# A list scheduler for the feed-forward work of a fused attention, mixture and ELU kernel; PSUM banks that sum on between reads

## The chip, the core and the metric

The kernel runs on one core of one Trainium2 chip. The metric is device time in microseconds (us) of one execution. A core has five instruction queues that run side by side, each strictly in its written order: PE (matrix products), DVE and POOL (elementwise work), ACT (copies and activation functions, which also may issue DMAs) and SP, which here issues nearly all DMAs. A queue whose first instruction waits holds everything behind it.

## The reference, cut to what matters

```python
def _attn_ref(q, k, v):               # 2 x 8 heads, 1152 keys, 576 pooled queries, depth 64
    q_pool = q.reshape(B, H, S // 2, 2, D).mean(axis=3)
    attn = softmax(scale * q_pool @ k.T)
    return attn @ v                   # becomes x: 1152 tokens x 512
def _moe_ref(x, domain_probs, w1, w2):  # 4 experts, 512 -> 1024 -> 512
    p = domain_probs / (domain_probs.sum(-1, keepdims=True) + 1e-09)
    for e in range(E):
        out += p[:, e:e + 1] * (np.maximum(x @ w1[e], 0.0) @ w2[e])
def _moe2_ref(x, w_in, w_out):        # 512 -> 2048 -> 512, weights are 64-bit floats
    h = x @ w_in
    g = np.where(h > 0.0, h, np.exp(np.minimum(h, 0.0)) - 1.0)
    return g @ w_out
```

## The kernel before

**Stages.** Attention comes first and is not touched: its instructions stand on every engine in the same order in both kernels. Then come twelve groups of feed-forward work, each for 512 hidden columns: groups 0 to 7 are the four experts (two groups each, ReLU), groups 8 to 11 the ELU network. G1 = 8 is the first ELU group. The output of groups 0 to 7, summed in `acc`, is the input x of groups 8 to 11.

**The two products of a group.** The first one (512 to 512) is made by seven products of quarter matrices instead of eight, numbered 1 to 7, each for two halves s of its 576 tokens. TURNS is the order of the seven. Such a product (i, s) is 12 matmuls of 288 columns: two output halves, two contraction chunks, and three matmuls each, since every float32 operand is kept as a rounded high part and a low rest (h and l in the names), and high x high, low x high and high x low are summed. The hidden values are sums of the seven products: quarter 2 is p1+p2, 3 is p1+p6+p5+p3, 7 is p1+p6+p7+p5, 4 is p1+p6+p7-p4 (the numbers name the product that ends each). The second product (512 to 512) goes by six blocks (b, m), three token blocks b by two output halves m, each 24 matmuls of 384 columns. Both go through `product`, so all these matmuls bear one line, L877.

**What stands around the products.** `first` (L908 on) lets ACT copy p1 to `u0`; DVE adds the later products to `u0`, `u1`, `u2` (names u) and makes the hidden quarter in a tile `c`; ACT takes the ReLU of c as the high part `hh` (L890), DVE the low part `hl` (L891). Two PSUM buffers `ps1` serve all products, so a product can start only when the one two places before it has been read. For a block, DVE scales with the token's probability (`t`, L956) and POOL adds to `acc` (L957). Weights of the next group are split by ACT (L363, high) and POOL (L366, low; `sum` are the quarter sums).

**Narrowing.** The ELU weights come as 64-bit floats. `narrow(k)`, 32 steps in all, turns 512 columns into float32: one ACT instruction (L815), six DVE instructions (L816 to L832), one POOL sum (L835), a store to DRAM, and the load of the next 64-bit tile `d`, of which there is one. A step is written as one piece by `step`, so its six DVE instructions stand together, the first waiting for the load of `d`.

**Order.** Attention is ordered by a list scheduler (`order_of`). The feed-forward work is written by hand loops: product, its readers, and pieces of weight work from a list `pend`, two or one at a time. Narrowing steps stand after product 1 and after blocks with m = 0.

**The change of stage.** At g = G1 `split` and `combine_x` turn `acc` into the seven x operands, 1152 wide pieces (two chunks of 576 tokens) at a time, on ACT and DVE.

## Time and profile before

| what | value |
| --- | --- |
| median of 3 runs | 1065.26 us (1059.65 to 1066.82) |
| the profiled execution | 1059.69 us, span of its trace 1057.7 us |
| PE busy | 868.8 us (82%) |
| DVE busy | 644.8 us (61%) |
| POOL busy | 501.9 us (47%) |
| ACT busy | 403.2 us (38%) |
| mean granted clock of PE | 0.927 of full speed |

A trace shows when each instruction ran, what ended an engine's idle time (the releaser), and what clock PE was granted. Busy time of PE counts a matmul at a lower clock as longer, so a busy PE need not be a fast one. The rows below are copied from the views of this one execution; times in them count from its first instruction.

### The profile page before, as it was taken

What the parts mean: (1) busy time and instruction counts of PE and PEld (TensorE: products, weight loads), DVE (VectorE), ACT (ScalarE), POOL (GpSimd) and SP (SyncE); (2) the same over time, 40 slices, a digit from 0 to 9 for tenths busy, and PEclk for the clock granted to TensorE, in tenths of its full rate; (3) what the DMA queues carried; (4) which work ended last, traced back from release to release, by engine and by line L of the source; (5) the groups of instructions that cost most, each with busy time, mean ns of one, the idle gap of its engine ahead of it and who ended that gap; (6) DMA issues with size and microseconds to landing.
All of it is one profiled execution on the core that took longest, in us unless ns stands there. A gap on an engine that the chain in (4) does not pass through costs nothing.

```text
span 1057.7 us, 14469 instructions
## 1 busy us (share of the span) xinstructions
PE 868.8 (82%) x5470; PEld 791.1 (75%) x5470; DVE 644.8 (61%) x927; ACT 403.2 (38%) x816; POOL 501.9 (47%) x460
## 2 busy tenths in 40 slices
PE   8999999999596867958769598595865697988978
PEld 7777777776596867948669587595854597887978
DVE  8767786767555747567466574665756714436362
ACT  7777786775322213122121221212213344324140
POOL 4244333633325373563744637446375455536361
PEclk9999999999898998989979799897996699898989
DMA  7998787511412223222241222412221201102002
GB/s 240 190 177 182 191 177 178 103 45 46 161 48 76 92 89 117 61 60 90 72 140 47 73 81 65 157 36 84 82 59 41 79 1 40 41 1 80 1 1 90
DMA packets 48357, 95.02 MB, mean 90 GB/s; under 512 B 14368, under 2 KB 26144, under 8 KB 45344
## 3 DMA queue, kind: packets, MB, share of 16 engines
q1 hardware_dynamic: 48288, 94.11, 32.7%
q8 instruction: 43, 0.70, 0.3%
q14 instruction: 26, 0.21, 0.1%
HBM read 64.37 MB, written 10.84 MB: 71 GB/s over the span
## 4 chain that ended last, share of the span: by engine, by line
PE 44%; DVE 22%; DMA 10%; POOL 8%; issue 8%; ACT 7%; SPq 1%; DVEq 0%; ACTq 0%; POOLq 0%
PE p L877 26%; PE s L593 6%; PE t L655 5%; PE s L678 5%; DMA d<-in_va 4%; DMA d<-in_vb 3%; DVE c L366 3%; DVE nt L820 2%; DVE hl L891 2%; POOL sum L366 2%; DVE u L366 2%; DVE nt L823 2%; DMA acc<-xo 2%; POOL nt L835 2%; DVE e L902 2%
## 5 line engine op out<-in xcount | busy, mean ns | idle before, releaser
L877 PE MATMUL p<-hl,w2h 128*128 128x384 f32 x576 | 193.7, 336 | 4.7 <-POOL hl L906 4.7
L877 PE MATMUL p<-hh,w2h 128*128 128x384 f32 x576 | 194.1, 337 | 3.3 <-DVE t L956 3.1
L877 PE MATMUL p<-hh,w2l 128*128 128x384 f32 x576 | 193.1, 335 | 0.0
L877 PE MATMUL p<-XH,h 128*128 128x288 f32 x192 | 67.5, 352 | 90.4 <-DVE c L366 85.0
L957 POOL TENSOR_TENSOR acc<-acc,t 128x768 f32<-128x768 f32 x42 | 80.3, 1912 | 102.1 <-DVE t L956 102.1
L604 DVE TENSOR_REDUCE st<-s 128x1 f32<-128x512 f32 (+1 forms) x144 | 105.5, 751 | 18.6 <-PE s L593 15.2
L877 PEld LDWEIGHTS p<-XH,h 128*128 128x128 f32 x192 | 43.1, 225 | 96.3 <-DVE c L366 85.0
L593 PE MATMUL s<-K,Q 128*128 128x320 f32 (+1 forms) x480 | 110.1, 356 | 4.5 <-DVE xo L363 2.6
L877 PEld LDWEIGHTS p<-hl,w2h 128*128 128x128 f32 x576 | 108.7, 189 | 5.8 <-POOL hl L906 5.8
L877 PEld LDWEIGHTS p<-hh,w2h 128*128 128x128 f32 x576 | 108.6, 188 | 5.9 <-DVE t L956 5.3
L877 PEld LDWEIGHTS p<-hh,w2l 128*128 128x128 f32 x576 | 108.7, 189 | 0.0
L610 ACT ACTIVATE e<-s,st 128x512 f32<-128x512 f32 (+1 forms) x144 | 106.4, 747 | 5.6 <-DVE st L604 3.5
L363 ACT CAST h<-sum 128x512 fp32r<-128x512 f32 x48 | 29.7, 620 | 184.7 <-POOL sum L366 184.7
L366 POOL TENSOR_TENSOR l<-sum,h 128x512 fp32r<-128x512 f32 x48 | 62.9, 1311 | 75.2 <-ACT h L363 75.2
L877 PE MATMUL p<-K,h 128*128 128x288 f32 x384 | 81.8, 307 | 19.6 <-DVE u L366 8.1
L655 PE MATMUL t<-ident,e 128*128 128x128 f32 x648 | 94.1, 276 | 3.4 <-ACT e L610 2.5
L835 POOL TENSOR_TENSOR nt<-nt,ne 128x512 f32<-128x512 f32 x32 | 40.9, 1277 | 117.4 <-DVE ne L832 72.4
L655 PEld LDWEIGHTS t<-ident,e 128*128 128x128 f32 x648 | 75.4, 140 | 24.3 <-issue 7.4
L890 ACT ACTIVATE hh<-c 128x576 fp32r<-128x576 f32 x64 | 43.9, 685 | 128.1 <-DVE c L366 128.1
L891 DVE SCALAR_TENSOR_TENSOR hl<-c,hh 128x576 fp32r<-128x576 f32 x64 | 59.2, 925 | 53.6 <-ACT hh L890 53.6
L593 PEld LDWEIGHTS s<-K,Q 128*128 128x128 f32 x480 | 74.0, 190 | 11.3 <-DVE xo L363 3.0
L877 PEld LDWEIGHTS p<-K,h 128*128 128x128 f32 x384 | 64.5, 197 | 21.9 <-ACT u L923 8.3
(103 smaller groups left out, 1989.0 us busy)
## 6 DMA issues: line engine op xcount, KB each, us to landing
w<-in_wb SPq DMA_DIRECT2D x8, 1024.0 KB, 4.8
d<-in_va SPq DMA_DIRECT2D x16, 512.0 KB, 3.9
w<-nt SPq DMA_DIRECT2D x32, 256.0 KB, 2.6
d<-in_vb SPq DMA_DIRECT2D x16, 512.0 KB, 4.5
w<-w SPq DMA_DIRECT2D x8, 1024.0 KB, 4.9
Q<-q SPq DMA_DIRECT2D x28, 288.0 KB, 6.2
w<-in_wa SPq DMA_DIRECT2D x7, 1024.0 KB, 4.8
v<-in_v SPq DMA_DIRECT2D x16, 288.0 KB, 5.9
```

The costliest lines, as they stand in the source:

```text
L363: (nc.scalar.copy if e == "ACT" else engines[e].tensor_copy)(out, a)
L366: engines[e].tensor_tensor(out=out, in0=a, in1=b, op=op)
L593: nc.tensor.matmul(out=t[:, j], lhsT=q[:, o : o + P], rhs=ks[p % 2][:, y, c : c + PARTS[z][1]], start=k == x == 0, stop=2 * k + x == last,)
L604: nc.vector.tensor_reduce(out=nm[b, z], in_=s_t[b, z], axis=AX.XY, op=ALU.max, negate=True)
L610: nc.scalar.activation(et[b % NP][:, part(z)].rearrange("p (j k) -> p j k", j=PARTS[z][0]), s_t.pop((b, z)), AF.Exp, bias=nm.pop((b, z)), ...
L655: nc.tensor.transpose(t[:, c * P : c * P + P], et[b % NP][:, (3 * u + c) * P : (3 * u + c + 1) * P], ident)
L678: nc.tensor.matmul(out=tb[i, h][64 * z : 64 * z + 64, :HQ], lhsT=raws[i, "v"][:, c, :], rhs=pt[i % 2][:, c, half(z)], start=c == cs[0], st ...
L835: nc.gpsimd.tensor_tensor(out=t, in0=t, in1=e, op=ALU.add)
L877: nc.tensor.matmul(out=ps, lhsT=w[a][:, c, m * P : m * P + P], rhs=x[b][:, c], start=c == a + b == 0, stop=c == cs - 1 and a == 1,)
L890: nc.scalar.activation(oh, c, AF.Relu)
L891: nc.vector.scalar_tensor_tensor(out=ol, in0=c, scalar=0.0, in1=f(oh), op0=ALU.max, op1=ALU.subtract)
L957: nc.gpsimd.tensor_tensor(out=o, in0=o, in1=t, op=ALU.add)
```

## The change

The hand loops are replaced by a second list scheduler. `ffn_ops` writes every piece of feed-forward work as an operation: the engines it may run on with a duration in ns, what it needs, a due time taken from a plan of PE's products, and what buffer it takes or gives back. `ffn_order` then picks, again and again, the ready operation that can start first, by due time where several can, and the kernel is recorded in that order. Letters: F a product, P a block, u the copy of a partial sum, c a whole quarter, r and l its high and low part, t and a the scaling and the sum into acc, s h o the first weights (sum, high, low), C L the second weights, W Z D p loads, N a narrowing step's nine parts, H Y T the x operands, n e w x the ELU.

Four things change in the work itself. Product 6 sums on in the PSUM bank of product 1, then 7, then 4, and product 3 in that of 5; between them ACT copies the bank (u), so that PE must wait for that copy before it adds the next product. The eight additions that DVE made for each half of a group become three (c) and ACT makes three copies instead of one. Narrowing is issued in single instructions between others. The PSUM is four tiles of two banks that products and blocks share, with three tiles c and three tiles t. The x operands at the change of stage are made in halves of 576 elements, some on POOL. Weights and low parts of groups 8 to 11 may go to DVE instead of POOL, and the first load of second weights is issued by ACT. In groups 1 to 7 and 9 to 11 the order of products is 1, 2, 6, 7, 4, 5, 3.

```diff
--- before.py
+++ after.py
...
+FREE = dict(PE=0, DVE=13000, ACT=3000, POOL=6000, SP=15000)
+BUSY = dict(PE=0, DVE=75, ACT=85, POOL=30, SP=0)
+SEEN = dict(PE=200, DVE=40, ACT=40, POOL=40, SP=0)
+LATE_X = 15500
+PACE = 11600
+NARROW = [
+    dict(ACT=650), dict(DVE=830), dict(DVE=1200), dict(DVE=430), dict(DVE=690), dict(DVE=430),
+    dict(DVE=690), dict(POOL=1300), dict(SP=350),
+]
+HALF = {2: (0, 1), 3: (0, 0), 7: (1, 0), 4: (1, 1)}
...
+    for key in plan:
+        g = key[1]
+        if key[0] == "F":
+            i, s = key[2:]
+            need = [prev, ("o", g, i), ("Y", g, i, s)]
+            need += {6: [("u", g, 1, s)], 7: [("u", g, 6, s)], 4: [("u", g, 7, s)], 3: [("c", g, 7, s)]}.get(i, [])
+            last = {1: 4, 5: 3, 2: 2}.get(i)
+            op(key, dict(PE=1592), need, begin[key], takes=last and "ps")
+        else:
+            _, g, b, m, z = key
+            need = [prev] + [("L", g, c) for c in range(4)]
+            for j in range(384 * b // 288, (384 * b + 383) // 288 + 1):
+                need += [("l", g, q, j % 2) for q in HALF if HALF[q][1] == j // 2]
+            op(key, dict(PE=4162 if z == 2 else 2081), need, begin[key], takes="ps")
+        prev = key
...
+                if q in (2, 3, 7):
+                    need = {2: [src, ("u", g, 1, s)], 3: [src, ("u", g, 6, s)], 7: [("u", g, 7, s), ("F", g, 5, s)]}[q]
+                    hold = begin["F", g, 5, s] if q == 2 and turns[g][1] == 2 else nxt[3] if q == 7 else 1 << 40
+                    give = [] if q == 7 else [("ps", ("F", g, {2: 2, 3: 5}[q], s))]
+                    src = ("c", g, q, s)
+                    op(src, dict(DVE=755), need, min(due, hold - 800), takes="c" if q != 7 else None, gives=give)
+                    give = [("c", ("u", g, 7, s) if q == 7 else src)]
+                else:
+                    give = [("ps", ("F", g, 1, s))]
+                if g < G1:
+                    op(("r", g, q, s), dict(ACT=660), [src], due + 1000)
+                    op(("l", g, q, s), dict(DVE=755), [("r", g, q, s)], due + 1700, gives=give)
...
+    for k in range(8 * (NG - G1)):
+        at = 2000 + PACE * k
+        op(("D", k), dict(SP=350), [("N", k - 1, n) for n in (0, 1, 6)], at - 6000, lag=6500)
+        for n, on in enumerate(NARROW):
+            need = {
+                0: [("D", k), ("N", k - 1, 8)], 1: [("D", k), ("N", k - 1, 7)], 2: [("N", k, 0)],
+                4: [("N", k, 3), ("N", k, 1)], 7: [("N", k, 4), ("N", k, 6)],
+            }.get(n, [("N", k, n - 1)])
+            op(("N", k, n), on, need, at + PACE + 600 * n, after=at if n < 2 else 0, lag=4500 if n == 8 else 0)
...
+    while ready:
+        best = []
+        for o, t in ready.items():
+            x = ops[o]
+            pool = x["takes"]
+            if pool:
+                if not pools[pool]:
+                    continue
+                t = max(t, min(pools[pool].values()))
+            _, e = min((max(t, free[e]) + n, e) for e, n in x["on"].items())
+            best.append((max(t, free[e]), x["due"], place[o], o, e))
+        start, _, _, o, e = min(best)
+        x = ops[o]
+        del ready[o]
+        free[e] = start + x["on"][e] - BUSY[e]
+        end[o] = start + x["on"][e] + SEEN[e] + x["lag"]
...
-    TURNS = [(1, 5, 6, 7, 3, 2, 4)] + [(1, 2, 5, 6, 7, 4, 3)] * (NG - 1)
+    TURNS = [(1, 2, 6, 7, 4, 5, 3)] * NG
+    TURNS[0], TURNS[G1] = (1, 5, 6, 7, 3, 2, 4), (1, 2, 5, 6, 7, 4, 3)
...
+    part_sums = {i: bc_p.tile([P, 2, 2, SB], F32, name="u%d" % i) for i in (1, 6)}
+    banks = [ps_p.tile([P, 2, 512], F32, name="p%d" % j) for j in range(4)]
+    cs = [bc_p.tile([P, 2, SB], F32, name="c%d" % j) for j in range(3)]
+    ts = [bc_p.tile([P, 2, NB], F32, name="t%d" % j) for j in range(3)]
...
+    def psum(g, i, s):
+        return runs[{6: 1, 7: 1, 4: 1, 3: 5}.get(i, i), s][:, :, :SB]
+
+    def first(e, g, i, s, n=None):
+
+        if n is not None:
+            runs[i, s] = banks[n]
+        x = [t[:, :, sub(s)] for t in right[i]]
+        for m in range(2):
+            product(psum(g, i, s)[:, m], wt[g, i], x, 2, m, n is not None)
+
+    def keep(e, g, i, s, n=None):
+        if n is not None:
+            kept[7, s] = cs[n]
+        nc.scalar.copy(kept[7, s] if i == 7 else part_sums[i][:, s], psum(g, i, s))
+
+    def whole(e, g, q, s, n=None):
+        if n is not None:
+            kept[q, s] = cs[n]
+        if q == 7:
+            tt(e, kept[7, s], psum(g, 5, s), kept[7, s], ALU.add)
+        else:
+            tt(e, kept[q, s], psum(g, q, s), part_sums[{2: 1, 3: 6}[q]][:, s], ALU.add)
...
-            if g == G1:
-                split(1)
-                split(2)
-            for y, i in enumerate(TURNS[g]):
-                for z in range(2):
-                    first(g, i, z)
...
-                if y == 0:
-                    step(4 * g - 1)
-                    pend += conv_ops(g)
-                some(1)
...
-            for b, n in enumerate(BLOCKS if g == 0 else BLOCKS[::-1]):
-                for m in range(2):
-                    second(g, n, m)
-                    if m == 0:
-                        step(4 * g + b)
-                    if b or m:
-                        some(2)
...
+        for _, _, (x, *k), e, n in ffn_order(ffn_ops(NG, G1, TURNS)):
+            do[x](e, *k, *([] if n is None else [n]))
```

DVE at the start of an expert group, before: a narrowing step (L816 to L832, d is its 64-bit tile) and then c, the sums that empty the two PSUM buffers p1 of product 2.

```order
L816 TENSOR_SCALAR ne_4184<-d_4120 128x512
L820 TENSOR_SCALAR nt_4183<-nt_4183 128x512
L823 TENSOR_SCALAR nt_4183<-nt_4183 128x512
L828 TENSOR_TENSOR nt_4183<-nt_4183,ne_4184 128x512
L829 TENSOR_SCALAR ne_4184<-nt_4183 128x512
L832 SCALAR_TENSOR_TENSOR ne_4184<-d_4120,ne_4184 128x512
L366 TENSOR_TENSOR c_4211<-p1_4198,u0_2694 128x576
L891 SCALAR_TENSOR_TENSOR hl_2691<-c_4211,hh_2690 128x2x288
L366 TENSOR_TENSOR c_4228<-p1_4215,u0_2694 128x576
L891 SCALAR_TENSOR_TENSOR hl_2691<-c_4228,hh_2690 128x2x288
```

DVE at the same place after; t2 is the last block's scaling, the L10xx lines are narrowing, p3 and p1 here are the PSUM tiles of product 2.

```order
L604 TENSOR_TENSOR t2_2706<-p1_2698,pb_2676 128x768
L1037 TENSOR_SCALAR ne_2679<-d_2677 128x512
L1042 TENSOR_SCALAR nt_2678<-nt_2678 128x512
L1046 TENSOR_SCALAR nt_2678<-nt_2678 128x512
L1051 TENSOR_TENSOR nt_2678<-nt_2678,ne_2679 128x512
L604 TENSOR_TENSOR c0_2701<-p3_2700,u1_2695 128x576
L1053 TENSOR_SCALAR ne_2679<-nt_2678 128x512
L1057 SCALAR_TENSOR_TENSOR ne_2679<-d_2677,ne_2679 128x512
L604 TENSOR_TENSOR c2_2703<-p1_2698,u1_2695 128x576
L1135 SCALAR_TENSOR_TENSOR hl_2692<-c0_2701,hh_2691 128x2x288
```

The narrowing step that stood whole ahead of both c now has its last two parts between them, and the low parts hl follow after both.

ACT at the same place before: u0 are the copies of product 1, hh the ReLU of quarter 2, L815 narrowing, h and w2h weights.

```order
L923 COPY u0_2694<-p1_4150 128x576
L923 COPY u0_2694<-p1_4164 128x576
L363 CAST h_4179<-sum0_73 128x512
L815 ACTIVATE nt_4183<-d_4120 128x512
L363 CAST w2h_2688<-w_3923 128x512
L890 ACTIVATE hh_2690<-c_4211 128x2x288
L890 ACTIVATE hh_2690<-c_4228 128x2x288
L363 CAST h_4232<-w_3921 128x512
```

ACT after: u1 are the copies of product 1, hh the ReLU of quarter 2, and u6 the copies of the bank after product 6.

```order
L601 CAST w2h_2689<-w_4519 128x512 x4
L1113 COPY u1_2695<-p3_2700 128x576
L601 CAST wh2_83<-sum1_74 128x512
L1113 COPY u1_2695<-p1_2698 128x576
L1035 ACTIVATE nt_2678<-d_2677 128x512
L1130 ACTIVATE hh_2691<-c0_2701 128x2x288
L601 CAST wh3_85<-sum0_73 128x512
L1130 ACTIVATE hh_2691<-c2_2703 128x2x288
L1113 COPY u6_2696<-p3_2700 128x576
L1113 COPY u6_2696<-p1_2698 128x576
```

New are the two u6 copies, which product 7 needs, and they stand behind the ReLU of both halves of quarter 2.

DVE at the change of stage before: the end of a narrowing step, the last block's scaling, the x operands XL (products 1 and 5) and K (product 2) with a difference in acc, then the next step.

```order
L832 SCALAR_TENSOR_TENSOR ne_6554<-d_6485,ne_6554 128x512
L956 TENSOR_TENSOR t_6591<-p2_6566,pb_5616 128x768
L366 TENSOR_TENSOR XL_71<-acc_72,XH_70 128x1152
L366 TENSOR_TENSOR K1_76<-acc_72,K1_76 128x1152
L366 TENSOR_TENSOR acc_72<-acc_72 128x2x576
L366 TENSOR_TENSOR XL_71<-acc_72,XH_70 128x1152
L816 TENSOR_SCALAR ne_6635<-d_6564 128x512
L820 TENSOR_SCALAR nt_6634<-nt_6634 128x512
L823 TENSOR_SCALAR nt_6634<-nt_6634 128x512
L828 TENSOR_TENSOR nt_6634<-nt_6634,ne_6635 128x512
```

DVE at the change of stage after: K0 are the low parts of x for product 3, xl that for product 6, c2 and c1 the quarter 2.

```order
L1042 TENSOR_SCALAR nt_2678<-nt_2678 128x512
L604 TENSOR_TENSOR acc_72<-acc_72 128x2x288
L1046 TENSOR_SCALAR nt_2678<-nt_2678 128x512
L604 TENSOR_TENSOR K0_75<-acc_72,K0_75 128x2x288
L1051 TENSOR_TENSOR nt_2678<-nt_2678,ne_2679 128x512
L604 TENSOR_TENSOR K0_75<-acc_72,K0_75 128x2x288
L1053 TENSOR_SCALAR ne_2679<-nt_2678 128x512
L604 TENSOR_TENSOR c2_2703<-p3_2700,u1_2695 128x576
L1057 SCALAR_TENSOR_TENSOR ne_2679<-d_2677,ne_2679 128x512
L604 TENSOR_TENSOR c1_2702<-p1_2698,u1_2695 128x576
L604 TENSOR_TENSOR acc_72<-acc_72 128x2x288
L604 TENSOR_TENSOR xl_2647<-acc_72,xh_2646 128x2x288
```

The low parts of x are halved, and the last steps of narrowing stand between them; xl for product 6 follows a whole step.

## Rows read from the trace of the kernel before

**Rows 1.** Stretches: length; busy us (count) of PE, PEld, DVE, ACT, POOL; clock; DMA.

```profile
0.00:253.60 253.60, 243.84 (x1726) 187.87 (x1726) 185.85 (x345) 185.62 (x472) 107.11 (x181) 1.00 0.70 155
253.60:319.70 66.10, 52.17 (x313) 50.59 (x314) 40.65 (x52) 16.82 (x26) 18.64 (x15) 0.92 0.33 104
448.60:515.20 66.60, 50.81 (x314) 48.88 (x313) 41.48 (x54) 15.11 (x25) 35.34 (x26) 0.92 0.26 79
489.50:515.20 25.70, 25.25 (x146) 24.93 (x145) 15.03 (x21) 4.26 (x7) 13.71 (x10) 1.00 0.21 62
467.50:472.50 5.00, 4.97 (x24) 4.67 (x24) 3.52 (x4) 2.40 (x4) 2.41 (x3) 0.65 0.59 148
783.20:875.20 92.00, 59.08 (x315) 56.88 (x314) 49.25 (x51) 33.90 (x48) 50.40 (x32) 0.80 0.10 35
875.20:935.80 60.60, 52.20 (x313) 50.20 (x312) 26.99 (x33) 21.70 (x34) 31.23 (x23) 0.94 0.10 35
897.90:901.20 3.30, 3.22 (x12) 2.90 (x12) 1.72 (x3) 1.75 (x3) 1.72 (x2) 0.51 0.56 169
...
1054.30:1057.70 3.40, 0.01 (x1) 0.00 (x0) 0.56 (x1) 0.00 (x0) 0.00 (x0) 1.00 0.16 58
```

**Rows 2.** Timeline of PE: start, us, first and last matmul of product 1.

```profile
515.20 0.29 PE L877 MATMUL p<-XH,h 128*128 128x288 f32 x1
...
518.25 0.29 PE L877 MATMUL p<-XH,l 128*128 128x288 f32 x1
```

**Rows 3.** Waits from 448 to 516: who waited for whom, us, times, longest.

```profile
PE p L877 <- DVE c L366: 11.0, 1, 11.0
PE p L877 <- DVE u L366: 3.2, 3, 2.0
```

**Rows 4.** The chain that ended last, 448 to 516, in order of time.

```profile
459.31 3.85 DMA d<-in_va
...
466.12 0.69 DVE ne L832
466.81 0.68 DVE c L366
```

**Rows 5.** Groups of instructions by shape, whole span: busy us, mean ns, idle before.

```profile
L957 POOL TENSOR_TENSOR acc<-acc,t 128x768 f32<-128x768 f32 x42 | 80.3, 1912 | 102.1 <-DVE t L956 102.1
L366 POOL TENSOR_TENSOR w2l<-w,w2h 128x512 fp32r<-128x512 f32 x48 | 63.8, 1338 | 12.3 <-ACT w2h L363 12.3
L366 DVE TENSOR_TENSOR c<-p,u 128x576 f32<-128x576 f32 x72 | 54.0, 750 | 39.7 <-PE p L877 39.2 <-issue 0.5
L890 ACT ACTIVATE hh<-c 128x576 fp32r<-128x576 f32 x64 | 43.9, 685 | 128.1 <-DVE c L366 128.1
L835 POOL TENSOR_TENSOR nt<-nt,ne 128x512 f32<-128x512 f32 x32 | 40.9, 1277 | 117.4 <-DVE ne L832 72.4 <-PE p L877 23.1 <-issue 21.9
L956 DVE TENSOR_TENSOR t<-p,pb 128x768 f32<-128x768 f32 x42 | 39.4, 953 | 17.7 <-PE p L877 17.7
L363 ACT CAST w2h<-w 128x512 fp32r<-128x512 f32 x48 | 28.4, 614 | 12.7 <-DMA w<-in_wb 12.7
L832 DVE SCALAR_TENSOR_TENSOR ne<-d,ne 128x512 f32<-128x512 uint32 x32 | 22.2, 693 | 1.1
L923 ACT COPY u<-p 128x576 f32<-128x576 f32 x24 | 14.6, 635 | 41.7 <-PE p L877 41.7
L829 DVE TENSOR_SCALAR ne<-nt 128x512 uint32<-128x512 uint32 x32 | 13.7, 427 | 1.1
```

**Rows 6.** Timelines of DVE and POOL: start, us; an instruction that overlaps one of the other.

```profile
519.86 2.03 POOL L957 TENSOR_TENSOR acc<-acc,t 128x768 f32<-128x768 f32 x1
520.22 1.95 DVE L823 TENSOR_SCALAR nt<-nt 128x512 uint32<-128x512 uint32 x1
...
468.12 1.28 POOL L366 TENSOR_TENSOR w2l<-w,w2h 128x512 fp32r<-128x512 f32 x1
468.23 1.78 DVE L891 SCALAR_TENSOR_TENSOR hl<-c,hh 128x576 fp32r<-128x576 f32 x1 [0.75 <-ACT hh L890]
471.43 0.76 DVE L891 SCALAR_TENSOR_TENSOR hl<-c,hh 128x576 fp32r<-128x576 f32 x1 [0.75 <-ACT hh L890]
```

## What I expect, and why

> **What bounds the kernel now.** I read the stretches first [rows 1]. Attention ends at 253.6 us with the clock at 1.00 throughout; the change does not touch it. From there to 1054.3 the feed-forward groups run, and 3.4 us of scaling and storing follow. One expert group (448.6 to 515.2) takes 66.6 us, an ELU group 60.6, the first ELU group, which waits for the change of stage, 92.0. To judge these I need what PE must do. Product 1 of both halves is 24 matmuls whose first and last start 3.05 us apart [rows 2]: 0.1326 us each, 1.59 for a product, 22.3 for fourteen. The six blocks of a group fill 489.5 to 515.2, busy 25.25 at full clock [rows 1]. A group is therefore 47.5 us of PE work, twelve are 570, and 800.7 are used. The 230.7 us in between are what a new order can give back.
>
> The waits say where they are [rows 3]: in this expert group PE waits once for 11.0 us for a c of DVE, and 3.2 us for sums that empty PSUM buffers. The chain says why [rows 4]: a load of a 64-bit tile d lands after 3.85 us, the six DVE instructions of that narrowing step follow (the last at 466.12), and only then the c for which PE waits. After it PE runs at clock 0.65 for 24 matmuls, 5.0 us instead of 3.2 [rows 1]. So an expert group is bound by one in-order queue, DVE, on which a DMA wait stands ahead of work that PE needs.
>
> **The expert groups 1 to 7.** With four PSUM tiles and the narrowing instructions moved, no load stands ahead of a c that PE needs soon: by the order, the load of the next d is issued after the sixth DVE part and its first reader stands several operations later. That removes the 11.0 and the 1.8 of clock after it. The 3.2 for emptied buffers goes too, since two more buffers stand ready. What is late next has to be found among DVE, POOL and ACT.
>
> DVE and POOL block each other. A POOL sum runs from 519.86 to 521.89; a short DVE instruction that came at 520.22 ends at 522.17 [rows 6], 0.28 after it, though such a one takes 0.43 alone (the row of L829 [rows 5]). A low part hl that came at 468.23 ends 0.61 after the POOL instruction it met (469.40), and a free one takes 0.76 [rows 6]. So an instruction with its operands in SBUF waits until the other's is done, and all but 0.15 us of it counts. The additions c and scalings t read PSUM, and I count them as free of it, from the c rows' mean of 750 ns [rows 5].
>
> In an expert group the claims add up so: POOL has 19 instructions of 1.28 us (15 of weights, 4 of narrowing) and 6 sums of 1.91 [rows 5], 35.8, as its busy 35.34 says [rows 1]. DVE has four narrowing steps of four short (0.28) and two long parts (0.69 less 0.15), 8.8, and six low parts from SBUF at 0.61, 3.7. Together 48.3 us against 47.5 of PE. Neither has room to be late.
>
> So I walk the start of such a group along the new order, in us from its first matmul. DVE scales the last block until 1.2. POOL makes the first low part from 0.8 to 2.1, so narrowing part 1 ends at 2.4. POOL's sum into acc goes to 4.2, part 2 to 4.5, the next low part to 5.7, part 3 to 6.0, the next to 7.2, part 4 to 7.8. The first c of quarter 2 reads PSUM and ends at 8.5, part 5 meets a low part and ends at 9.3, part 6 at 10.0 (POOL's own narrowing part waits for it), the second c at 10.7. ACT stands with the ReLU of this c (0.69) ahead of the first u6 copy (0.64) [rows 5], which ends at 12.0. Product 7 adds to the bank that this copy reads, and PE could begin it after six half products, at 9.5. PE waits 2.5 us. The end of the group is late as well: from the first block on POOL has nine short ones and five sums (21.1) and DVE two narrowing steps and four low parts (6.9), 28.0 in 25.25; POOL and DVE come about 2 us late into the next group, where the same wait grows to 4.5. A wait of 3.2 us also brings the clock down (0.51 in 897.9 to 901.2, 12 matmuls in 3.30 [rows 1]), but those 1.7 fall mostly into time that DVE needs anyway. I take 47.5 + 4.5 = 52.0, for seven groups 364. Bounds: 48.5 if the instructions pass between each other better than my strict alternation, 59 if each of DVE's 30 such instructions waits the 1.02 that the slow hl row shows over the free one: own time 28.7 (narrowing 12.4, low parts 6.1, c 4.5, t 5.7, by [rows 5, 6]) plus 30.6.
>
> The Trainium skill, "SBUF — State Buffer", section "SBUF: two separate sides", says that the port pair which DVE and POOL share is locked for the whole instruction. By that the claims would be 52.2 instead of 48.3, and the sum some 4 us a group higher. The two meetings in [rows 6] show 0.15 us of a DVE instruction outside the lock.
>
> **Group 0.** The order is bound there by ACT and DVE rather than PE. The four high parts of the second weights (0.61 each [rows 5]) stand ahead of the copy that the second c of quarter 7 needs, and product 3 sums on in the bank that this c reads: 1.7 us. Before the first block seven short and low instructions stand between the fourth product's x operand and the last low part, 4.3 us on DVE with one POOL instruction between, of which 0.7 are covered by the second half of product 4: 4.6. With 0.7 for the operand itself, 47.5 + 7.0 = 54.5 instead of 66.1.
>
> **The change of stage, group 8.** The halved operands for products 1, 2 and 5 are made under the last three blocks (12.6 us), so the idle time at its start goes. Product 6 needs two differences and a split after the very last sum into acc, and on DVE a whole narrowing step and two c stand in between: by the same alternation its low part ends at 15.4, where PE could start at 9.5; its second half costs 2.2 more. Later two more narrowing steps stand between the c of quarter 7 and product 3 (5.6), and this group keeps product 4 late, so that the ELU chain of five instructions is waited for ahead of the first block (4.8, [rows 5] durations). 47.5 + 17.5 = 65.0 instead of 92.0.
>
> **Groups 9 to 11.** Narrowing is over. Product 4 comes ahead of 5 and 3 now: four half products, 6.4 us, cover a chain of min, exp, max, high and low of five times some 0.7 us and two c of 0.75, which ends 0.4 us before it is needed. I take 48.0 a group, 144 in all, instead of 60.6 for the one shown.
>
> **The sum.** 253.6 + 54.5 + 364 + 65 + 144 + 3.4 = 884.5 us of span. Around the span the profiled execution has 2.0 (1059.69 against 1057.7): 886.5. The median of the runs is 0.5% above the profiled one (1065.26), so 890.
>
> **Rivals.**
> 1. PE is the bound. POOL often waits for inputs, and DVE's instructions find the port free; then expert groups take 48.5 (-24.5), group 8 58 (-7), group 0 51 (-3.5): 851.5, by the same half per cent 856. For it: in the old trace the two met rarely, and POOL was idle for half of each group. Against it: the port sum above.
> 2. The port is the bound. DVE pays the 1.02 us of the slow hl row at each of 30 instructions, groups take 59 (+49): 935.5, 940 as a median. The Trainium skill's rule above ("SBUF — State Buffer") leans this way. Against: POOL would have to have work ready at each of those moments.
> 3. The change of stage does not do what it says: the halves still wait for the whole of acc, group 8 stays at 92 (+27): 913.5, 918.
> 4. Slower than before: the load of d stands ahead of PE's work in more than one of the four steps. One such wait cost 11.0 and 1.8 of clock; from two a group on (26 x 7 = 182 more) the gain is eaten, 1068.5, 1074 as a median. Against: by my walk each load has some 5 us or more before its first reader, and 3.85 were needed [rows 4].
>
> **Chances and range.** My forecast 0.52, rival 1 0.26, rival 2 0.16, rival 3 0.04, rival 4 0.02. Everything but the last is faster by far more than 1%, which is about what a measurement can tell from no change here: faster 0.97, same 0.01, slower 0.02. The range goes from 850, just under rival 1, to 932, towards rival 2; below and above I leave about a tenth each.
>
> **What will show it.** PE's waits: no wait over 6 us for c in the expert groups, instead one of 2 to 5 us per group for u6 ahead of product 7, released by ACT. Expert groups of 50 to 54 us, ELU groups of 47.5 to 49, the first ELU group 60 to 70. DVE's narrowing parts should show a mean near 1 us for the short ones while POOL is over 65% busy in expert groups. I would be wrong if PE waits for POOL (first weights, port) at a group's start, or if a load of w arrives late because two of a megabyte are queued one behind the other.

## The result, and the profile after

The changed kernel takes 903.54 us (median of 4, 898.47 to 906.51), the kernel before 1066.04 beside it (1059.65 to 1068.0): a ratio of 0.848, 95% interval 0.843 to 0.853. The profiled execution took 903.64, its span is 901.9. The forecast was 890, in a range of 850 to 932.

The stretches of the kernel after, in the columns of [rows 1]: attention, group 0, groups 1 to 7 together, one expert group, the first ELU group, the next one, the tail.

```profile
0.00:259.43 259.43, 246.41 (x1726) 189.89 (x1727) 186.18 (x345) 185.67 (x472) 106.99 (x181) 0.99 0.67 152
259.43:316.84 57.41, 50.69 (x312) 49.89 (x313) 41.35 (x50) 21.57 (x36) 24.21 (x18) 0.94 0.37 120
316.84:675.45 358.61, 340.63 (x2186) 337.04 (x2185) 288.05 (x297) 120.04 (x203) 269.71 (x170) 0.98 0.31 104
364.09:416.53 52.44, 49.23 (x314) 48.60 (x313) 43.23 (x44) 18.14 (x31) 38.16 (x24) 0.97 0.29 100
675.45:753.63 78.18, 56.17 (x314) 53.75 (x313) 62.73 (x67) 31.00 (x51) 44.86 (x27) 0.85 0.18 61
753.63:803.13 49.50, 47.89 (x314) 47.26 (x314) 33.66 (x43) 21.50 (x36) 13.13 (x8) 1.00 0.11 43
898.50:901.90 3.40, 0.00 (x0) 0.00 (x0) 0.45 (x1) 0.00 (x0) 0.00 (x0) 1.00 0.16 58
```

An expert group fell from 66.6 to a mean of 51.2 (358.61 by seven), the first ELU group from 92.0 (87.0 from its first matmul on, after PE had stood for 4.8) to 78.2, the others from some 60 to 48.3 (144.9 for three). Against the terms of the prediction's sum: attention +5.8, group 0 +2.9, groups 1 to 7 -5.4, group 8 +13.2, groups 9 to 11 +0.9, tail 0: +17.4 on 884.5.

Who PE waits for in groups 1 to 7, which answers [rows 3] (there for one group):

```profile
PE p L1090 <- POOL wl L604: 13.5, 6, 3.0
PE p L1090 <- DVE c L604: 1.5, 1, 1.5
PE p L1090 <- ACT u L1113: 1.4, 1, 1.4
```

The 11.0 us for c are gone. What PE waits for now is `wl`, the low part of a first weight that POOL makes, once in each of groups 2 to 7, and always ahead of product 6 (the matmul is `p<-xh,wl`). Group 1, in which no step begins in the first 6 us, takes 47.2 and has no such wait. Groups of instructions by shape, in the columns of [rows 5], show how DVE and POOL stretch each other:

```profile
L604 POOL TENSOR_TENSOR acc<-acc,t 128x768 f32<-128x768 f32 x42 | 86.2, 2055 | 19.9 <-DVE t L604 19.9
L1051 DVE TENSOR_TENSOR nt<-nt,ne 128x512 uint32<-128x512 uint32 x32 | 39.8, 1244 | 0.6
L604 DVE TENSOR_TENSOR c<-p,u 128x576 f32<-128x576 f32 x48 | 35.8, 749 | 7.1 <-PE p L1090 6.6
L1053 DVE TENSOR_SCALAR ne<-nt 128x512 uint32<-128x512 uint32 x32 | 32.3, 1009 | 0.6
L1035 ACT ACTIVATE nt<-d 128x512 f32<-128x512 f32 x32 | 21.5, 670 | 125.2 <-DMA w<-nt 113.4 <-POOL acc L604 11.9
```

L1053 is what L829 was: 427 ns before [rows 5], 1009 now. c, which reads PSUM, stays at 750. The last row has a wait of which the prediction says nothing: the first part of a narrowing step, on ACT, stands for 113.4 us in all until the step before has been stored from `nt`, of which there is one.

The chain that ended last at the start of group 2 (its first matmul is at 364.09), in order of time:

```profile
360.45 1.30 POOL nt L1061
...
361.77 3.36 DMA w<-nt
...
365.23 0.68 ACT nt L1035
...
365.94 0.44 DVE nt L1042
...
366.40 0.43 DVE nt L1046
366.83 0.86 DVE t L604
...
368.57 1.97 DVE ne L1053
```

And the timelines of DVE (first three rows) and POOL there: start, us.

```profile
364.54 1.09 DVE L1037 TENSOR_SCALAR ne<-d 128x512 uint32<-128x512 uint32 x1 [2.43 <-DMA d<-in_vb]
...
366.74 0.95 DVE L604 TENSOR_TENSOR t<-p,pb 128x768 f32<-128x768 f32 x1
...
370.56 0.69 DVE L1057 SCALAR_TENSOR_TENSOR ne<-d,ne 128x512 f32<-128x512 uint32 x1
...
371.33 1.27 POOL L1061 TENSOR_TENSOR nt<-nt,ne 128x512 f32<-128x512 f32 x1 [1.09 <-DVE ne L1057]
372.55 1.26 POOL L604 TENSOR_TENSOR wl<-sum,wh 128x512 fp32r<-128x512 f32 x1
```

Read down: a step's sum is stored (3.36), only then may ACT begin the next step; DVE's first part has waited 2.43 for d at the same time, and the scaling t of the last block stands behind it on DVE, so that it runs 2.65 us after the group's start. POOL's sum into acc, the narrowing sum and then `wl` follow; PE needed `wl` at 370.9 and goes on at 373.87.

So it is in groups 2 and 6, where t starts 2.65 and 4.43 us after the group's first matmul. In group 5 (1.32) t stands behind the last part of the step before. In groups 3, 4 and 7 it starts at 0.27, and PE waits 2.65, 0.35 and 2.58 us for `wl` all the same. DVE (t and L1046) and POOL in group 3, whose first matmul is at 416.53:

```profile
416.80 0.96 DVE L604 TENSOR_TENSOR t<-p,pb 128x768 f32<-128x768 f32 x1 [0.59 <-PE p L1090]
...
421.86 1.95 DVE L1046 TENSOR_SCALAR nt<-nt 128x512 uint32<-128x512 uint32 x1
...
417.02 1.29 POOL L1061 TENSOR_TENSOR nt<-nt,ne 128x512 f32<-128x512 f32 x1
...
421.51 2.01 POOL L604 TENSOR_TENSOR acc<-acc,t 128x768 f32<-128x768 f32 x1
423.49 1.45 POOL L604 TENSOR_TENSOR w2l<-w,w2h 128x512 fp32r<-128x512 f32 x1
424.90 1.70 POOL L604 TENSOR_TENSOR wl<-sum,wh 128x512 fp32r<-128x512 f32 x1
```

Here POOL works without a pause from 414.82 until `wl`, which starts 8.37 us after the first matmul: the sum of the step before and a sum into acc are left over from group 2 and stand ahead, and the new step's parts stretch what follows.

In group 8 PE stands from the end of product 2 to 695.67 for the c that empties its PSUM tile. DVE there (start, us), and the matmul of PE that waited:

```profile
684.67 2.03 DVE L1037 TENSOR_SCALAR ne<-d 128x512 uint32<-128x512 uint32 x1
686.62 1.49 DVE L1042 TENSOR_SCALAR nt<-nt 128x512 f32<-128x512 f32 x1
688.03 1.95 DVE L604 TENSOR_TENSOR acc<-acc 128x576 f32<-128x576 f32 x1
...
691.51 1.95 DVE L604 TENSOR_TENSOR K<-acc,K 128x576 fp32r<-128x576 f32 x1
693.38 1.48 DVE L1053 TENSOR_SCALAR ne<-nt 128x512 uint32<-128x512 uint32 x1
694.78 0.74 DVE L604 TENSOR_TENSOR c<-p,u 128x576 f32<-128x576 f32 x1
...
695.67 0.58 PE L1090 MATMUL p<-XH,wh 128*128 128x288 f32 x1 [11.81 <-DVE c L604]
```

Narrowing parts stand between the halves of the x operands, most of them stretched by POOL (the three that are not shown took 0.41 to 0.74), with c last.

### The profile page after: what moved, and what is told of

It is laid out like the page before. It is cut to its first block, busy times and chain, and to the rows that moved or that the text cites. A ratio compares the mean times of both kernels' runs of the same rounds, so it can differ in the third digit from the quotient of the medians.

```text
span 901.9 us, 14280 instructions
## 1 busy us (share of the span) xinstructions
PE 836.9 (93%) x5470; PEld 772.2 (86%) x5470; DVE 678.9 (75%) x891; ACT 414.9 (46%) x853; POOL 471.8 (52%) x410
## 4 chain that ended last, share of the span: by engine, by line
PE 50%; DVE 24%; DMA 10%; POOL 6%; issue 5%; ACT 3%; SPq 1%; ACTq 0%; DVEq 0%; POOLq 0%
PE p L1090 31%; PE s L815 7%; PE s L900 6%; PE t L877 6%; DMA w<-nt 4%; DVE nt L1051 3%; DVE ne L1053 3%; DVE nt L1046 2%; DVE hl L1135 2%; DMA acc<-xo 2%; POOL acc L604 2%; POOL nt L1061 2%; DVE c L604 2%; DVE nt L1042 2%; DVE t L1151 1%
## 5 line engine op out<-in xcount | busy, mean ns | idle before, releaser
L815 PE MATMUL s<-K,Q 128*128 128x320 f32 (+1 forms) x480 | 112.1, 361 | 8.5 <-DVE xo L601 3.8
L832 ACT ACTIVATE e<-s,st 128x512 f32<-128x512 f32 (+1 forms) x144 | 106.3, 746 | 6.1 <-DVE st L826 3.8
L604 POOL TENSOR_TENSOR acc<-acc,t 128x768 f32<-128x768 f32 x42 | 86.2, 2055 | 19.9 <-DVE t L604 19.9
L815 PEld LDWEIGHTS s<-K,Q 128*128 128x128 f32 x480 | 75.4, 193 | 15.8 <-DVE xo L601 4.2
L1090 PE MATMUL p<-K,wh 128*128 128x288 f32 x384 | 79.7, 301 | 8.9 <-DVE c L604 6.7
L604 POOL TENSOR_TENSOR st<-st,st 128x5 f32<-128x5 f32 (+2 forms) x80 | 19.2, 249 | 119.6 <-DVE st L848 82.4
L1035 ACT ACTIVATE nt<-d 128x512 f32<-128x512 f32 x32 | 21.5, 670 | 125.2 <-DMA w<-nt 113.4
L900 PE MATMUL s<-pt,v 128*64 128x288 f32 x576 | 76.7, 412 | 0.0
L1061 POOL TENSOR_TENSOR nt<-nt,ne 128x512 f32<-128x512 f32 x32 | 44.5, 1390 | 60.3 <-DVE ne L1057 60.3
L601 ACT COPY pt<-t 128x384 f32<-128x384 f32 (+1 forms) x125 | 55.2, 456 | 42.7 <-PE t L877 38.7
L604 POOL TENSOR_TENSOR wl<-w,wh 128x512 fp32r<-128x512 f32 x35 | 52.9, 1523 | 40.3 <-ACT wh L601 40.3
L601 DVE COPY pt<-t 128x384 f32<-128x384 f32 (+1 forms) x115 | 56.2, 501 | 22.2 <-PE t L877 18.3
L1090 PE MATMUL p<-xh,wl 128*128 128x288 f32 x192 | 60.0, 313 | 13.5 <-POOL wl L604 13.5
```

What stands on the lines that cost most here:

```text
L601: (nc.scalar.copy if e == "ACT" else engines[e].tensor_copy)(out, a)
L604: engines[e].tensor_tensor(out=out, in0=a, in1=b, op=op)
L815: nc.tensor.matmul(out=t[:, j], lhsT=q[:, o : o + P], rhs=ks[p % 2][:, y, c : c + PARTS[z][1]], start=k == x == 0, stop=2 * k + x == last,)
L832: nc.scalar.activation(et[b % NP][:, part(z)].rearrange("p (j k) -> p j k", j=PARTS[z][0]), s_t.pop((b, z)), AF.Exp, bias=nm.pop((b, z)), ...
L900: nc.tensor.matmul(out=tb[i, h][64 * z : 64 * z + 64, :HQ], lhsT=raws[i, "v"][:, c, :], rhs=pt[i % 2][:, c, half(z)], start=c == cs[0], st ...
L1035: nc.scalar.activation(nt, hi.bitcast(F32), AF.Abs)
```

## The experiments

Three theories stood at the start. **Queue:** the gain comes from taking the whole narrowing step away from in front of c on DVE, where the load of d made it late. **Port:** what remains is lost because DVE and POOL exclude each other. **Cover:** the ELU groups gain because product 4 comes earlier and covers their chain. The load theory is the part of the first that blames the load of d; after e7 and e9 came a theory of **place**, that it matters where in a group a step begins, not how many there are. The table has all kernels; a group's length is from first matmul to first matmul in the profiled execution (the last one's to PE's last matmul), "1 to 7" is the mean, "9 to 11" the sum. By this measure the 4.8 us for which PE stands at the old change of stage count to group 7.

| kernel | median us | ratio to before [95%] | group 0 | 1 to 7 | 8 | 9 to 11 |
| --- | --- | --- | --- | --- | --- | --- |
| before | 1066.04 | 1 | 66.0 | 66.9 | 87.0 | 179.1 |
| after | 903.54 | 0.848 [0.843, 0.853] | 57.4 | 51.2 | 78.2 | 144.7 |
| before, step later (e1) | 1072.51 | 1.011 [1.006, 1.016] | 66.0 | 68.7 | 86.3 | 177.6 |
| after, step whole (e2) | 910.77 | 0.857 [0.852, 0.861] | 54.7 | 52.2 | 79.8 | 145.0 |
| after, no narrowing (e3) | 856.42, one run | | 55.6 | 47.3 | 66.3 | 146.3 |
| after, weights of 6 first (e4) | 907.33 | 0.854 [0.850, 0.858] | 59.0 | 52.2 | 78.2 | 143.2 |
| before, d loaded once (e5) | 1050.55, one run | | 67.5 | 65.5 | 87.0 | 177.7 |
| after, 29 to 31 held (e6) | 887.10 | 0.834 [0.831, 0.837] | 56.3 | 51.4 | 65.3 | 144.2 |
| after, pace 15 (e7) | 902.53 | 0.848 [0.845, 0.851] | 57.4 | 51.1 | 68.2 | 154.0 |
| after, old turns (e8) | 917.28 | 0.863 [0.860, 0.867] | 57.4 | 51.7 | 78.9 | 159.9 |
| after, d loaded once (e9) | 887.55, one run | | 57.4 | 50.1 | 78.1 | 144.8 |
| before, no narrowing (e10) | 953.41, one run | | 66.0 | 52.8 | 78.9 | 180.8 |
| two d, two t, held (e11) | 902.25 | 0.850 [0.846, 0.853] | 57.7 | 51.9 | 68.7 | 155.1 |
| free start (e12) | 886.26 | 0.835 [0.831, 0.839] | 57.4 | 48.1 | 68.9 | 163.8 |

**e1: in the kernel before, the step of product 1 moved behind the last product.**

```diff
-                if y == 0:
+                if y == 6:
                     step(4 * g - 1)
+                if y == 0:
                     pend += conv_ops(g)
```

> The kernel before with one edit: the narrowing step that stood behind product 1 stands behind the last product of the group. Nothing else is changed. Queue theory (the gain in groups 1 to 7 is that no load stands ahead of a c that PE needs): the wait of 11.0 us and the 1.8 us of low clock after it go in groups 1 to 8, expert groups fall from 66.6 to 53 to 56 us, the time from 1066 to 965 to 985 us. PSUM theory (the gain is the chain, the fewer DVE additions and the shared tiles): the load's wait moves ahead of another sum of DVE, groups stay above 62 us, the time above 1030 us.

1.1% slower. In an expert group (455.4 to 525.7) PE's waits, in the columns of [rows 3], became

```profile
PE p L877 <- DVE c L366: 6.8, 2, 4.3
PE p L877 <- DVE t L956: 6.5, 1, 6.5
```

The products got shorter (40.9 to 36 us), the blocks longer (25.7 to 32 to 34): a whole step stops PE in this place too. One other place does not give the gain.

**e2: the six DVE parts of a step put together again, where the last of them stood.**

```diff
-    return sorted(out)
+    out = sorted(out)
+    last = {x[2][1]: n for n, x in enumerate(out) if x[2][0] == "N" and x[2][2] == 6}
+    at = lambda n, x: last[x[2][1]] + (x[2][2] - 6) / 10 if x[2][0] == "N" and 1 <= x[2][2] <= 6 else n
+    return [x for _, x in sorted((at(n, x), x) for n, x in enumerate(out))]
```

> The kernel after with the six DVE parts of every narrowing step put together at the place of the sixth, all else in its order. Queue and port theory: a whole step of 3 us, with POOL instructions between its parts up to 8 us, stands in one piece where c and low parts stood between the parts; PE gets waits of 1 to 4 us for DVE in every expert group: 51.2 us a group become 53 to 57, the time 915 to 945 us. Rival (single steps matter little, since the total claim on the port is the same and POOL's weights set the pace): expert groups within 1 us of 51.2, the time 896 to 911 us.

1.0 us a group, 7 in all, with intervals that still overlap by a little. That narrowing goes in single instructions is worth little. What is left for the gain of the expert groups is where the scheduler puts a step and what PE can do meanwhile, with four PSUM tiles.

**e3 and e10: both kernels without the work of narrowing on DVE and POOL.**

```diff
+            if x == "N" and 0 < k[1] < 8:
+                continue
```

> The kernel after without parts 1 to 7 of narrowing (its six DVE instructions and the POOL sum are left out, so the ELU weights are wrong numbers; loads, the ACT part and stores stay). Port theory: without 13.9 us of claims on the shared port per group the low part of product 6's weights is in time, no wait of PE over 0.6 us is left in groups 1 to 7, they take 47.3 to 48.2 us; group 8 falls from 78 to 58 to 64 us; time 855 to 870 us. Order theory (product 6's weights come late since their buffer is freed only by product 1, and four POOL instructions stand ahead): waits of 1.5 to 3 us ahead of product 6 stay, groups 49.5 to 51, time 880 to 895 us.

For e10 lines L816 to L835 of the kernel before were taken out.

> The kernel before without the six DVE instructions and the POOL sum of each narrowing step (the ELU weights are wrong); ACT's part, loads and stores stay. Theory that the place of narrowing is nearly all: the 11.0 us wait, the slow clock after it and the port's share go, an expert group falls from 66.6 to 50 to 54, the whole to 930 to 965. Theory that the PSUM buffers and the eight additions weigh as much: the group stays at 56 or more, since PE waits for sums that empty two buffers, the whole at 980 or more.

The stretch of groups 1 to 7 without narrowing, in the columns of [rows 1], after (e3) and before (e10):

```profile
307.39:638.35 330.96, 330.96 (x2186) 330.80 (x2186) 141.63 (x146) 121.60 (x204) 220.59 (x146) 1.00 0.35 113
```

```profile
318.36:688.20 369.84, 343.66 (x2185) 335.95 (x2185) 168.68 (x210) 107.67 (x177) 205.28 (x145) 0.99 0.33 104
```

After, PE does not pause once: 47.3 a group, so that 47.5 as the floor was right. Narrowing therefore costs 3.9 a group after (51.2 less 47.3) and 14.1 before (66.9 less 52.8): 10.2 of the 15.7 won in a group are that narrowing costs less. How much of that is its place and how much the shared PSUM tiles, which may let PE go on while DVE is late, was not parted. The other 5.5 are the chained sums, the tiles and the new turns together (52.8 to 47.3; e8 gives the turns 0.5); PE's waits in e10 are 18 for sums u, 20.1 us in all, as [rows 3] had 3.2 in one group. In group 0 and the ELU groups narrowing explains nothing: 66.0 and 180.8 without it.

**e4: high parts of the weights of products 7 and 4 only after that of 6.**

```diff
+        if i in (7, 4) and 0 < g != G1:
+            need = need + [("h", g, 6)]
```

> The kernel after with one more need in the planner: the weights of products 7 and 4 of groups 1 to 7 and 9 to 11 wait for those of product 6, so that product 6's pair is made under the blocks of the group before. Order theory: the waits for POOL ahead of product 6 (13.5 us in groups 1 to 7, some 4 of low clock behind them) go, expert groups 48.5 to 49.5 us, time 883 to 893 us. Port theory: the port is as full as before, the same lateness comes out at the next product (7 or 4, or the copies u6 ahead of 7), groups 50.5 to 52, time 898 to 906 us.

The wait for `wl` is gone, and the time is not. PE's waits in groups 1 to 7:

```profile
PE p L1092 <- ACT u L1115: 15.7, 7, 5.3
PE p L1092 <- DVE c L606: 8.7, 2, 7.8
```

Now PE waits for the u6 copy ahead of product 7, the place that the prediction named. The first wait had hidden the second: with one gone, the other shows. (Of the 8.7 for c, 7.8 are one wait in group 5.)

**e5: the kernel before with d loaded once.**

```diff
-            wd[k] = t
+            wd.update(dict.fromkeys(range(8 * (NG - G1)), t))
...
-                load_d(k + 1)
```

> The kernel before with only the first load of d; the other 31 loads of 64-bit tiles are left out, so every narrowing step works on the first tile and the ELU weights are wrong. All instructions of DVE, POOL, ACT and PE stay where they were; only the wait for the load goes. The experiment with the moved step showed the load's wait coming out at another place, so this takes all of them away at once. Load theory (the 66.6 us of an expert group are the waits for loads in front of PE's work, and the new order wins because no load is waited for): expert groups 52 to 56 us, time 960 to 990 us. Buffer theory (two PSUM tiles for products and two for blocks, emptied by a DVE that makes eight additions per half, hold PE whatever comes in time): expert groups stay above 61 us, time above 1020 us.

The wait for c is still 10.8 us in each group from 397 us on. The chain up to that c:

```profile
454.95 1.80 POOL acc L957
456.75 1.41 POOL sum L366
...
458.18 0.62 ACT h L363
458.80 0.57 ACT nt L815
...
459.40 1.04 DVE nt L820
...
462.11 0.69 DVE ne L832
462.80 0.68 DVE c L366
```

So the load was not the cause that [rows 4] seemed to show. With it the step's last part starts 17.5 us after the group's first matmul (466.12 in [rows 4], less 448.6), without it 17.15 (462.11 less 444.96): another chain ends less than 0.4 us before. ACT's part of the step stands behind a weight copy (`h`) that waits for a sum on POOL, that for POOL's sum into acc, and DVE's whole step stands ahead of c. The queue part of the theory holds, its load does not.

**e6: steps 29 to 31 held until the first block of group 8.**

```diff
-        op(("D", k), dict(SP=350), [("N", k - 1, n) for n in (0, 1, 6)], at - 6000, lag=6500)
+        held = [("P", G1, 2, 0, 2)] if k == 29 else []
+        op(("D", k), dict(SP=350), [("N", k - 1, n) for n in (0, 1, 6)] + held, at - 6000, lag=6500)
```

> The kernel after with the narrowing steps 29 to 31 held back until the first block of group 8 is done, so that no narrowing stands in the product part of group 8. Port theory (in group 8 the narrowing parts and the POOL instructions they meet delay the c of quarter 2, for which product 5 waits 11.8 us): group 8 falls from 78.2 to 66 to 70 us, near the 66.3 without any narrowing; group 9 takes 49 to 52; time 890 to 897 us. Rival (PE waits there for the chain of x operands on POOL and ACT, and narrowing fills gaps): group 8 above 75 us, time 899 to 906 us.

Group 8 falls by 12.9 us, and nothing is given back in groups 9 to 11. Its stretch, in the columns of [rows 1]:

```profile
671.80:737.12 65.32, 51.58 (x313) 49.73 (x313) 55.23 (x65) 31.22 (x51) 34.51 (x20) 0.92 0.16 57
```

**e7: a narrowing step planned each 15.0 us instead of 11.6 (PACE).**

> The kernel after with a narrowing step every 15.0 us of the plan instead of 11.6: three steps instead of four in most expert groups, the rest in groups 9 and 10, where the weights go to DVE and POOL is nearly idle. Port theory: 3.5 us less of claims in an expert group (44.8 against 47.5 of PE): expert groups 48 to 50 us instead of 51.2, group 8 as before (74 to 79), group 9 49 to 52; time 884 to 895 us. Rival (each step costs PE its wait wherever it stands, and the waits of ACT for the store of the step before decide): the gain of groups 1 to 7 is lost again in 9 and 10, time 898 to 907 us.

22 steps lie in groups 1 to 7 instead of 26, and a group takes 51.1 as before: four steps fewer buy nothing there. Group 8 gains 10.0, groups 9 to 11 lose 9.3: the last steps stand beside the ELU chain there, and PE waits 5.1 for hh and 2.0 for hl. The number of steps is not what an expert group pays for.

**e8: the old order of products, 1, 2, 5, 6, 7, 4, 3, from group 1 on.**

> The kernel after with the products of groups 1 to 7 and 9 to 11 in the order of before (1, 2, 5, 6, 7, 4, 3). Cover theory (in ELU groups the chain of five instructions behind product 4 is hidden because two products, 6.4 us, follow it): with one product behind it, ELU groups take 49.5 to 51 us instead of 47.5, and in expert groups product 6's weights have 3.2 us more, so that no wait for POOL is left ahead of it and they take 49 to 51; time 895 to 912 us. Rival (the order of products matters little, since the block of the other token range covers the chain): ELU groups within 0.5 us of 47.5, time within 5 us of 903.

Groups 9 to 11 lose 15.1 (PE waits 5.2 for hh and 6.6 for hl ahead of blocks), the expert groups 0.5 each. The cover is real, and worth more than was expected; the rest of the gain in the ELU groups (180.8 to 159.9, narrowing apart) belongs to the other changes together: the chained sums, the tiles, and the weights and low parts that may go to DVE.

**e9: the kernel after with d loaded once.**

```diff
     def load_d(e, k):
+        if k:
+            return
```

> This leaves out the loads of d after the first, so that all 32 narrowing steps work on the first tile (the ELU weights are wrong); every instruction on DVE, POOL and ACT stays where it was. Load theory: in the changed kernel DVE still stands at d for 1 to 3 us at the start of most expert groups, with the scaling t of the last block behind it, POOL's sum into acc and the low part for product 6 behind that; without the loads PE's 13.5 us of waits for POOL vanish, groups 1 to 7 fall from a mean of 51.2 to 48 to 49.5, and the whole to 880 to 893. Port theory: the six DVE instructions, stretched by POOL's, are what delays the low part; groups stay at 50.5 to 52, the whole at 897 to 906.

Between the two theories: 1.1 us a group. PE still waits 9.0 us for `wl`, 5 times, instead of 13.5. The load of d is 1.1 of the 3.9 us that a group loses to narrowing; without it ACT's part still waits 88.7 us in these groups, 13 times, for the store from `nt` (101.2, 17 times, in the kernel after), and the parts still stand where they stood. (8.2 of the 16.0 us by which this run is shorter lie in attention.)

**e11: two tiles d, paid for with two t instead of three, on top of e6.** The load of step k waits for step k - 2.

> The version that holds steps 29 to 31 (887.1) with two tiles d, so that the next load goes out a whole step earlier, paid for with two tiles t instead of three. Load theory: groups 1 to 7 fall from a mean of 51.4 there to 48.5 to 50, the whole to 866 to 880. Port theory: 884 to 890, no change. Third possibility: two tiles t are too few, a scaling waits for POOL's sum in every block, and the whole is 890 or more.

The third possibility: 15 us slower than e6. DVE does not wait for d any more in groups 1 to 7, but PE's waits for `wl` are still 10.4 us there, and those for c rise to 7.8. The load alone is not the lever. Groups 8 to 11 lose 14.3 of these us, 10.9 of them in groups 9 to 11, where PE waits 6.0 for hh (nowhere in e6) and where the ELU chain takes its tiles from the same two t. So the tiles are the likely cost; the two edits were not run apart.

**e12: no step begins over the start of a group.** Three steps begin in each of groups 1 to 7, after the low parts of quarter 2, and eight after the first block of group 8.

```diff
+            wait = []
+            if n < 2 and k >= 24:
+                wait = [("P", G1, 2, 0, 2)]
+            elif n < 2 and k % 3 == 0 < k:
+                wait = [("l", k // 3, 2, 1)]
-            op(("N", k, n), on, need, at + PACE + 600 * n, after=at if n < 2 else 0, lag=4500 if n == 8 else 0)
+            op(("N", k, n), on, need + wait, at + PACE + 600 * n, after=at if n < 2 else 0, lag=4500 if n == 8 else 0)
```

> No narrowing step begins between the last blocks of a group and the low parts of quarter 2 of the next: three steps lie in each of the groups 1 to 7, the other eight after the first block of group 8. Theory of place: what PE waits for in the expert groups is the one step that begins over the start of a group, ahead of the last scaling t; without it groups 1 to 7 take 47.3 to 49 instead of a mean of 51.2, group 8 takes 63 to 67, groups 9 and 10 give back 3 to 9 us together, and the whole is 865 to 885. Theory of amount: three steps claim the same port wherever they stand, a low part is late in another product, the groups stay at 50 to 51.5 and the whole at 885 to 895, by the gain of group 8 alone. The other side: eight steps in groups 8 to 10 delay the ELU chain by as much as is won, 895 to 905.

Groups 1 to 7 together, against e7 with nearly as many steps (21 here, 22 there), in the columns of [rows 1]; e12 first, with its groups 8 and 9:

```profile
310.46:647.31 336.85, 333.06 (x2186) 331.11 (x2185) 246.38 (x270) 117.62 (x197) 248.79 (x164) 1.00 0.29 99
647.31:716.19 68.88, 52.09 (x314) 50.20 (x314) 56.66 (x62) 31.24 (x51) 38.53 (x23) 0.93 0.19 65
716.19:774.35 58.16, 50.82 (x313) 49.64 (x313) 49.65 (x63) 22.90 (x38) 27.90 (x18) 0.94 0.23 78
```

```profile
313.78:671.46 357.68, 341.54 (x2185) 338.23 (x2185) 259.81 (x277) 117.59 (x198) 257.99 (x165) 0.98 0.28 95
```

20.8 us, at one step's difference: at three steps a group it is the place that decides. At the start of group 3 (first matmul at 406.22) DVE and POOL show

```profile
406.49 0.96 DVE L609 TENSOR_TENSOR t<-p,pb 128x768 f32<-128x768 f32 x1 [2.90 <-PE p L1095]
...
411.12 1.28 POOL L609 TENSOR_TENSOR wl<-sum,wh 128x512 fp32r<-128x512 f32 x1
```

t comes 0.27 us after the group's start, as it did in this group of the kernel after, but `wl` 4.9 instead of 8.4: no step's sum stands in POOL's queue, and no part of a step meets it. In group 2 t comes at 0.27 instead of 2.65, `wl` at 4.4 instead of 8.5. PE waits for POOL nowhere in these groups. But the steps saved there are paid for later: groups 8 to 11 take 232.6 against 209.5 in e6, 23.1 more, and the whole is level with e6 (886.26 and 887.10, intervals 0.831 to 0.839 and 0.831 to 0.837). Both beat the kernel after.

## Why the prediction was right in its size, and where it failed

**What it had right.** The range and the sign; PE's floor (47.5, e3 shows 47.3); that narrowing, not PE, bound the expert groups before (e10: they fall to 52.8); no wait over 6 us for c in the expert groups; the ELU groups (48.0 foreseen, 48.3 measured), with the cover as a part of the cause (15.1 of some 34, e8). Its sign of being wrong came true, though: PE waits for POOL, for first weights, near the start of six groups of seven. Three sums do not follow from their own terms: the waits of group 8 add up to 18.5 and not 17.5 (5.9, 2.2, 5.6, 4.8), the claims by the whole instruction to 52.8 and not 52.2, and the ELU chain ends 1.4 us and not 0.4 before it is needed (5.0 of 6.4).

**The expert groups: right size, wrong path.** 52.0 was forecast, 51.2 came. The step that failed is the walk along the order, from "DVE scales the last block until 1.2" on: it took the order at the start of one group for that of all seven. The order that the walk follows is that of group 4, and there it held: t at 0.27, `wl` done at 7.1, PE held up for 1.4 us by u6 ahead of product 7, where 2.5 was foreseen. In the other groups a step stands elsewhere. In groups 2 and 6 its first part waits for the load of d and its second for ACT, which waits for the store of the step before; t stands behind both. The walk held the load to have "some 5 us or more before its first reader" (rival 4), and had no term for the store at all. In groups 3, 5 and 7 the step before runs over the start, and its sum stands ahead on POOL; that "POOL and DVE come about 2 us late into the next group" was foreseen, but not that `wl` ahead of product 6 is held up by it sooner than u6 ahead of product 7. (By the walk's own times `wl` ends at 7.2, and PE asks for it at 6.8.) e4 shows that u6 was late too, just behind. That the size came out is in part luck: the sum had 4.5 us of waits and nothing for the clock, the trace has 2.6 idle and 1.2 of slower matmuls a group (340.63 busy by seven is 48.7).

The alternation of DVE and POOL is there: the four short narrowing parts have means of 0.83 to 1.06 us, where the prediction said near 1, and POOL is busy for 269.7 of 358.6 us. But it costs less than was summed. Where POOL runs without a pause in groups 1 to 7 of the kernel after, it is 1.25 us on average from the end of one instruction to the end of the next one on weights (or the next narrowing sum), if nothing of DVE ends in between or only a c or t. With a short narrowing part in between it is 1.44 (37 times), with a long one 1.69 (8 times), with a low part hl 1.76 (21 times). So they hold POOL up for 0.19, 0.45 and 0.52 us, where the prediction counted 0.28, 0.54 and 0.61; DVE's short part ends 0.28 to 0.36 after the POOL instruction that it met (43 times), as in [rows 6]. By these figures the claims of a group with four steps are 44.2 us (an estimate: 19 times 1.25 and 6 times 1.80 for POOL, 9.7 for DVE), not 48.3. The rule that the prediction quoted from the Trainium skill ("SBUF — State Buffer", section "SBUF: two separate sides") would have given some 4 us a group more; the trace does not bear that out, since POOL loses some 0.24 us less than the span of the DVE instruction each time.

So "neither has room to be late" was too strong: e7 takes away four steps and gains nothing, e12 one more and the place, and gains 3.0 a group. Whether four steps a group, placed as in e12, would also fit, was not tried.

**The cause in the kernel before.** The prediction read the 11.0 us from [rows 4] as a load standing ahead of c. e5 takes the load away and keeps 10.8. The rows showed the piece that ended last; e5 shows that the chain through POOL's sums and ACT ends less than 0.4 us ahead of it. The conclusion, that the step must not stand whole ahead of c, survived, because the wrong cause and the right one stood in the same place of the same queue; e1 shows that it is not cured by one move.

**Group 8, +13.2: a term that was mis-sized, in two parts.** The forecast added 17.5 us of waits to 47.5. The waits are 22.0 (78.18 less 56.17 busy), led by the 11.8 for the PSUM tile of product 2, a wait that the prediction did not have (it foresaw 5.9 ahead of product 6). The other part is the clock: PE is busy for 56.2 instead of 47.5, 8.7 us more, at 0.85. [rows 1] had shown 59.08 busy at 0.80 for the old group 8, and the sum left that out. e6 shows the cause of the larger wait: without the three steps in that place the wait for c is gone (6.8 us remain there, put down to ACT's xh), and the group takes 65.3, with 51.6 busy and 13.7 idle.

**Group 0, +2.9.** The waits are 6.7, the sum had 7.0. Again the clock was left out: busy 50.7 at 0.94.

**Attention, +5.8.** It was taken as fixed, and its order is. The first feed-forward matmul came at 253.6 in the trace of before, at 259.4 in that of after, and between 251.2 and 258.0 in the twelve experiments. In a sum against one profiled execution this is the noise to expect; the 0.5% for the median was of the same kind and did not come back (903.54 against 903.64).

**The rivals.** PE as the bound (48.5 a group) is what e12 comes to, in these groups alone. The port as a bound of 59 a group did not come. That the change of stage does nothing was wrong: 87.0 to 78.2 from the first matmul on, and the 4.8 us ahead of it are gone, though e10 has 78.9 in the old order without narrowing, so that what the halved operands bring alone was not separated. Several loads in PE's way: one a group, and 1.1 us, not 12.8.

## What to carry to other kernels

The row that ended last before a wait need not be its cause: where two chains end less than 0.4 us apart, as here, taking one away changes next to nothing (11.0 to 10.8), and only a run without it tells. A walk along the order of one group holds for that group; here one of seven had it at its start. A filler task with its own load, store and single buffer is best judged by what stands behind it in each queue where it begins, not by its total work: the same 21 or 22 steps cost 20.8 us more or less by place alone. And a stretch with long waits is to be summed at the clock that its old rows show, not at full clock.

## What was not expected of the hardware

The next write to a tile waits for the store that reads it: 3.36 us from the sum's end here, 113.4 us of ACT's idle time in all. After the 11.8 us wait in group 8 matmuls of 288 columns followed each other at 0.24 us instead of 0.13 (696.05 to 696.29), that is at 1.2 GHz instead of 2.4; the clock granted from 695.67 to 700 us was 0.50. In groups 1 to 7 of e3, where PE never paused, it was 1.00 for 331 us. And a DVE instruction that POOL met held it up for some 0.24 us less than its own span (0.19 of 0.43, 0.45 of 0.69, 0.52 of 0.76).
